# Cross-attention into a Winograd mixture layer on one core: a seventh product split once more, with placements, loads and transposes moved

## The chip, the cores and the metric

The kernel runs on one core of a Trainium2 chip. Its time is the device time of one execution in microseconds (us). The engines are TensorE (PE; PEld is its weight load), VectorE (DVE), ScalarE (ACT), GpSimd (POOL) and SyncE (SP), which here only issues DMAs. Each engine works through its own instructions in the order in which they were written; they meet only through semaphores. A DMA queue issues in order too.

## The reference

```python
x: (8, 8, 512, 64)   state: (8, 8, 32, 64)      # batch, head, tokens, features
scores = x @ state^T / 8;      a  = softmax(scores);   xread = a @ state
scores2 = state @ x^T / 8;     a2 = softmax(scores2);  sread = a2 @ x
t = concat([xread, sread], axis=tokens)                # (8, 8, 544, 64)
t = t.transpose(0, 2, 1, 3).reshape(4352, 512)
h = t @ w_in                                           # 512 x 2048
out = (h * sigmoid(h)) @ w_out                         # 2048 x 512
```

## The kernel before

The eight batches are worked through one after the other. For each batch b the 512 token rows of `xread` are never formed: W1[b] = state[b] @ w_in is made first (pieces of `ps_w`, line 479), and h = a @ W1[b] is sixteen tiles of 128 x 512 (`emit_G1`, line 546, two products of 512 columns each), put through SILU on ScalarE into `g` (line 574). The second matrix product, g @ w_out, is for batches 1 to 7 a Winograd form of Strassen's product: seven block products instead of eight, with p = 1 to 7 in `Unit.mm` (line 672), eight steps k of two 256-column products each. They need sums of halves of g on VectorE: `sums3` (in the code g's second half becomes a difference, in two instructions for k = 0 to 3 and 4 to 7), `sums2`, `sums1`, `sums4`; and differences of w_out, D1 to D4, made once (`t_weights`). Batch 0 uses plain products (`G2`, line 583). The last stage is the 256 rows of `sread`, at the end.

The seventh product (p = 7, the difference half of g with D3) is, for the batches named in INNER, split again by the same scheme (`inner_mm`, line 735): seven small products, each of four steps k of 128 columns. It needs four more sums of VectorE (`inner_sums`: t[2] from the first difference alone, t[0], t[1], t[3] from both), four weight differences made once in batch 1 (`inner_weights`, two on VectorE and two on GpSimd), and small copies and additions of VectorE that put the result together in `kept`. Inner product 1 reads only the first difference, 2 and 4 read the second.

The order within a batch is written out by hand. The loop over j (from 3 in batch 1 and 5 in the later ones, up to 15) emits h tile j, and `early(j)` puts behind it steps from the list `todo`, whose entries are (product, step, earliest j); products 1 and 7 are done there. At j = 5 and j = 9 the two differences of `sums3` are taken, and other VectorE work is put beside them. Then come products 2, 6, 4, 5 and 3, and between their steps the first five h tiles of the next batch (`units(3, {...})` says after which steps).

The attention of later batches is prepared ahead. With n = b + 1 and m = b + 2: x of batch m + 1 is loaded (`fetch_x`, on SP's queue), cast to bf16 by GpSimd (`cast_x`), transposed by a DMA (`transpose_x` into xT); scores of batch m are products (`scores_t`), exponentials on ScalarE (`exps_t`, into eT) are transposed by a DMA into e; `norm_t` sums them (reduction and reciprocal on VectorE), multiplies (half on GpSimd, half on VectorE), and `transpose_at` transposes the weights by a DMA into aT, which the h tiles of batch m read. Batch 2 is made in natural layout instead (`scores`, `exps`, `norm`, `transpose_a`). The states are loaded once, transposed by one DMA, and `evict_state` places them into stT, in four small copies for each half. State reads (`sread`) are done in groups, in batches 1, 4 and 6, normalised into xm, and transposed by DMAs (`transpose_xm`) for the last stage. `spread_x` copies x into the layout that the state reads take. ScalarE has to load a table whenever it changes between exponential and SILU.

Of the kernel before, what the change touches and what calls it, by code (L numbers as in the profile page):

```python
# [18 lines left out]
B = 8  # L19
# [23 lines left out]
def kernel(  # L43
# [8 lines left out]
    nc = tc.nc  # L52
# [58 lines left out]
    def load_x(b, h0=0, nh=H, eng=nc.gpsimd):  # L111
        eng.dma_start(
            x_f[b % 2][:, ds(h0, nh)],
            x[b, ds(h0, nh)].rearrange("h (p c) d -> p h c d", p=128, c=4)
        )
# [133 lines left out]
    def pe_transpose_x(b, hg, nb=2, new=bank, engs=(nc.vector, nc.scalar), only=None):  # L249
        if b not in xT:  # L250
            xT[b] = xtpool.tile([128, 4, 4, 128], BF16, tag="xT", name=f"xT{b}")
        m = 4 // nb
        for u in range(nb) if only is None else only:
            ps = new([128, m, 2, 128], BF16, "ps_xt")
            for i in range(m):
                for j in range(2):
                    nc.tensor.transpose(
                        ps[:, i, j, :],
                        x_nat[b][:, m * u + i, 2 * hg + j, :],
                        ident[:],  # L260
                    )
            copy(engs[u], xT[b][:, ds(m * u, m), ds(2 * hg, 2), :], ps[:])
# [23 lines left out]
    def evict_state(u, eng, b0, nb):  # L286
        to = stT.rearrange("p b k s (n m v) -> p b k s n m v", n=2, m=8)
        for g in range(2):
            for v in range(2):
                copy(  # L290
                    eng,
                    to[ds(64 * u, 64), ds(b0, nb), ds(2 * g, 2), u ^ g, :, :, v],
                    st_x[
                        ds(64 * v, 64), :, ds(b0, nb), ds(2 * g, 2), u, :
                    ].rearrange("p m b k n -> p b k n m"),
                )
# [62 lines left out]
    def norm_t(b):  # L359
        rs = att.tile([128, 2, 4, 4, 1], FP32, tag="rs2", name="rs2")  # L360
        rc = att.tile([128, 2, 4, 4, 1], FP32, tag="rcn", name="rcn")
        a = tpool.tile([128, 2, 4, 4, NS], BF16, tag="an2", name="an2")
        nc.vector.tensor_reduce(rs[:], e2[b][:], axis=AX, op=ADD)
        nc.vector.reciprocal(rc[:], rs[:])
        for hg, eng in enumerate((nc.gpsimd, nc.vector)):
            eng.tensor_tensor(
                a[:, hg], e2[b][:, hg], rc[:, hg].to_broadcast([128, 4, 4, NS]), op=MULT
            )
        return a

    def transpose_at(b, a):
        aT[b] = att.tile([128, 2, 4, 128], BF16, tag="aT", name="aT")
        nc.sync.dma_start_transpose(
            aT[b].rearrange("q g c p -> q (g c) p"), a.rearrange("p g c s n -> p (g c s n)")
        )
# [22 lines left out]
    def transpose_a(b, hg):  # L398
        nc.sync.dma_start_transpose(
            aT[b][:, hg, :, :], an[b, hg][:].rearrange("p c s n -> p (c s n)")  # L400
        )
# [174 lines left out]
    def G2(b, tt, ft):  # L576
        if ft == 0:
            if b == 0 and tt >= 2:
                outs[tt] = psA.tile([128, DM], FP32, tag=f"a{tt - 2}", name="o_a")
            else:  # L580
                i = 1 if b == B else tt % 2
                outs[tt] = psO.tile([128, DM], FP32, tag=f"o{i}", name="o")
        nc.tensor.matmul(  # L583
            outs[tt][:],
            gt[b * NFT + ft][:, ds(128 * tt, 128)],
            w_out_sb[:, ft, :],
            start=(ft == 0),
            stop=(ft == NFT - 1),
            skip_group_check=True,
        )  # L590
# [36 lines left out]
        }[which]  # L627
        sub(eng, d[which], a, c)

    INNER = (3, 4, 5, 6, 7)  # L630

    class Unit:
        def __init__(self, b):
# [262 lines left out]
    W0 = {2: (512, 512), 6: (1024, 512), 10: (1536, 512)}  # L896
    W1_AT = {2: 0, 6: 512}
    LEAD0 = [2, 3, 2, 2, 2, 3, 2, 1, 3, 3, 2, 3]
    T3 = {1: (0, 1), 2: (2,), 3: (3,), 4: (4,), 5: (5,), 6: (6,)}
    ready = 4  # L900
    for ft in range(12):
        upto(min(ft + LEAD0[ft], ready))
        if ft == 1:
            place_one_state(1, transpose_one_state(st1_n), nc.vector)
        if ft in W0:
            pss = w1_mms(0, [W0[ft]])
            if ft in W1_AT:
                pss1 = w1_mms(1, [(W1_AT[ft], 512)], new_h)
            w1_out(0, [W0[ft]], both, pss)
            if ft in W1_AT:  # L910
                w1_out(1, [(W1_AT[ft], 512)], both, pss1)
            ready = sum(W0[ft]) // 128
        if ft == 8:
            t_weights((1,), 0, 8)
        if ft == 9:
            t_weights((2, 3, 4), 0, 4)
        if ft == 11:
            for hg in range(2):
                cast_x(1, nc.gpsimd, 0, 2, 4 * hg, 4)
                cast_x(1, nc.vector, 2, 2, 4 * hg, 4)  # L920
            load_x(3)
            pe_transpose_x(1, 0, 1, engs=(nc.vector,))
            upto(16)
            nc.scalar.activation(warm[:], busy[:, 0:1], func=EXP, bias=0.0)
        for tt in range(3):
            G2(0, tt, ft)
            if ft == 7 and tt == 0:
                upto(9)
        for i in T3.get(ft, ()):
            G2(0, 3, i)  # L930
    pe_transpose_x(1, 1, 1, engs=(nc.vector,))
    G2(0, 3, 7)
    scores(1, 0, new=new_h)
    for ft in range(8, 12):
        G2(0, 3, ft)
    scores(1, 1, new=new_h)
    exps(1, 0)
# [48 lines left out]
    def fetch_x(i):  # L986
        n = 4 if i < 6 else H
        for h in range(0, H, n):
            load_x(i, h, n, nc.sync)

    for b in range(1, B):
        n = b + 1
        m = n + 1
        u = Unit(b)
        lead = 3 if b == 1 else LEADS
        inner = b in INNER
        if inner:
            todo = [(1, k - 8, k + 2) for k in range(6)] + [(7, 1, 9)]
            todo += [(7, 2, 10), (7, 4, 10), (7, 7, 11), (7, 6, 12), (7, 3, 13), (7, 5, 14)]
            todo += [(1, k - 8, 15) for k in (6, 7)]  # L1000
        else:
            last = 6
            todo = [(1, k - 8, k + 2) for k in range(last)]
            todo += [(7, k - 8, k + 4) for k in range(8)]
            todo += [(1, k - 8, k + 2) for k in range(last, 8)]
# [23 lines left out]
        for j in range(lead, NFT):  # L1029
            upto(NFT * b + j + 1)  # L1030
            if j == 8:
                u.hi = gh[b, 1]
            if j == max(lead, 5):
                u.sums3(0, 4)
                if b == 1:
                    t_weights((3,), 4, 4)
                    transpose_x(3)
                    for v in range(2):
                        evict_state(v, (nc.vector, nc.gpsimd)[v], 2, 2)
                if inner:  # L1040
                    u.inner_sums((3,))
                if 1 < b and m + 1 < B:
                    fetch_x(m + 1)
                if b == 2:
                    for v in range(2):
                        evict_state(v, (nc.vector, nc.gpsimd)[v], 4, 4)
            if j == 9:
                u.sums3(4, 4)
                if inner:
                    u.inner_sums((1, 2, 4))  # L1050
                if b == 1:
                    t_weights((2, 4), 4, 4)
                elif b == 2:
                    transpose_at(3, norm_t(3))
            early(j)
            if j == 13:
                u.sums2(0, 4)
        srs = SREAD_AT.get(b, ())

        def group_a():  # L1060
            pss = w1_next(PIECES_A[b])
            if m < B:
                scores_t(m)
            ps_sr = sread(srs, bank if m < B else new_h) if srs else None
            return pss, ps_sr
# [12 lines left out]
        if 2 < b < B - 1:  # L1078
            made = group_a()
# [3 lines left out]
        if 2 < b < B - 1:  # L1083
            xm = out_a()
# [23 lines left out]
            out_a()  # L1108
        if 1 < b and m < B:
            exps_t(m)  # L1110
        if b > 1 and srs:
            transpose_xm(srs, xm)
        step = 0

# [15 lines left out]
        if b == 1:  # L1130
            spread_x(2)
            for hg in range(2):
                norm(2, hg)
                transpose_a(2, hg)
            made = group_a()
            fetch_x(m + 1)
            exps_t(m)
            transpose_xm(srs, out_a())
        if m < B:
            nc.scalar.activation(warm[:], busy[:, 0:1], func=SILU, bias=0.0)  # L1140
        units(4)
# [20 lines left out]
        if b == 1:  # L1162
            group_b()
            for i in range(4):
                inner_weights(i, (nc.vector, nc.gpsimd)[i % 2])
        units(3, {2: 1, 3: 2, 5: 4, 7: 5} if b == 1 else {1: 2, 3: 3, 5: 4, 7: 5})
        if m + 1 < B:
            for c in range(4):
                cast_x(m + 1, nc.gpsimd, c, 1)
        if m == B:  # L1170
# [3 lines left out]
            normed = norm_t(m)  # L1174
        add(nc.vector, u.block(0, 1), u.block(0, 1), u.be[:])
        u.out_half(0)
        if m + 1 < B:
            transpose_x(m + 1)
        if 1 < b and m < B:
            transpose_at(m, normed)  # L1180
        for ft in range(NFT):
            gt.pop(NFT * b + ft)
    upto(NFT * B + NFT)
# [29 lines left out]
```

## Time and profile before

| | |
|---|---|
| median of 3 runs | 201.43 us (201.26 to 201.6) |
| profiled execution | 201.57 us, span 199.8 us |
| TensorE busy | 193.1 us, 97% of the span |
| VectorE busy | 157.1 us, 79% |
| ScalarE busy | 138.4 us, 69% |
| GpSimd busy | 72.7 us, 36% |
| mean granted TensorE clock | 0.998 of full speed |

Busy time is the sum of an engine's instructions. In the timelines, each line gives the start and the length in us from the start of the span, the engine, the line of the kernel, the operation, its output and inputs with their shapes, how many like it follow each other, and in square brackets how long the engine stood idle before it and what released it. Products overlap in TensorE's pipeline, so a line's length has some 0.16 us more than the distance to the next start; the distance between starts is what a product costs. VectorE's instructions overlap by about 0.08 us. In batch 2 product 2 begins near 69.7 us, in batch 3 at 91.59, in batch 4 at 113.14.

### The profile page before, as it was taken

The page shows a single profiled execution, that of the slowest core. Times are in us where ns is not written, and L with a number is a line of the kernel's source. Part 1 is how long each engine was busy: PE and PEld are TensorE (multiplying, and loading weights), DVE is VectorE, ACT ScalarE, POOL GpSimd, SP SyncE. Part 2 cuts the span into 40 slices and gives each one's busy share as a digit, 9 for nine tenths or more (in the row PEclk, how much of TensorE's full clock was granted, in tenths as well). Part 3 has the DMA queues.
Part 4 walks back from the last instruction along what each step waited for, and adds up shares of the span by engine and source line. Part 5 has one row for each costly group of instructions (what it writes and reads, how often), then busy time and mean ns, then how long its engine had stood idle before and what let it go on. Part 6 is the DMA issues. An engine that isn't in the chain of part 4 may idle for free.

```text
span 199.8 us, 4809 instructions
## 1 busy us (share of the span) xinstructions
PE 193.1 (97%) x1972; PEld 130.2 (65%) x1972; DVE 157.1 (79%) x289; ACT 138.4 (69%) x245; POOL 72.7 (36%) x93
## 2 busy tenths in 40 slices
PE   7799999999999999999999999999999999999992
PEld 2444445567766677667766777668666876788881
DVE  3852756997998999979998899989976997673072
ACT  3885657889777787889778957888588167825530
POOL 8664333750549803820273024602400226002200
PEclk9999999999999999999999999999999999999999
DMA  6999999993047998396229940842080005000042
GB/s 195 190 206 206 247 262 347 246 256 81 5 131 204 239 229 168 149 233 198 53 105 193 260 93 10 282 90 53 12 252 3 3 13 210 3 0 0 39 176 105
DMA packets 40822, 28.72 MB, mean 144 GB/s; under 512 B 27360, under 2 KB 37472, under 8 KB 40800
## 3 DMA queue, kind: packets, MB, share of 16 engines
q1 hardware_dynamic: 34592, 20.52, 39.2%
q0 software_dynamic: 5920, 7.64, 18.4%
q8 instruction: 15, 0.25, 0.5%
q10 hardware_dynamic: 288, 0.26, 0.4%
q14 instruction: 7, 0.06, 0.1%
HBM read 17.43 MB, written 8.91 MB: 132 GB/s over the span
## 4 chain that ended last, share of the span: by engine, by line
PE 85%; DMA 7%; DVE 5%; POOL 0%; issue 0%; POOLq 0%; DVEq 0%
PE o L672 34%; PE h L546 25%; PE ps_w L479 4%; DMA w_in_sb<-in_moe_w_in_dram 4%; PE h L564 3%; PE o L583 3%; PE o_a L583 3%; DMA xT<-x_nat 3%; PE o L735 2%; DVE g L597 2%; PE o_s L793 2%; PE o_ch L735 2%; PE o L793 1%; PE ps_sr L423 1%; DVE stT L162 1%; PE ps_scT L336 1%
## 5 line engine op out<-in xcount | busy, mean ns | idle before, releaser
L574 ACT ACTIVATE g<-h 128x512 bf16<-128x512 f32 (+1 forms) x142 | 79.9, 573 | 32.4 <-PE h L546 20.9
L546 PE MATMUL h<-aT,W 128*128 128x512 bf16 x252 | 72.9, 379 | 0.1
L672 PEld LDWEIGHTS <-g 128*128 128x128 bf16 x480 | 46.3, 98 | 22.4 <-DVE kept L600 0.7
L672 PE MATMUL o<-w_out_sb,g 128*128 128x256 bf16 x336 | 48.7, 273 | 0.1
L600 POOL TENSOR_TENSOR o_sb<-o_sb,kept 128x512 f32<-128x512 f32 x7 | 9.7, 1392 | 70.6 <-ACT o_sb L160 61.4
L546 PEld LDWEIGHTS <-W 128*128 128x128 bf16 x252 | 23.2, 98 | 7.9 <-issue 0.9
L672 PE MATMUL o<-wt,s 128*128 128x256 bf16 x224 | 27.3, 273 | 0.0
L162 DVE CAST W<-ps_w 128x512 bf16<-128x512 f32 (+1 forms) x35 | 21.7, 666 | 6.2 <-PE ps_w L479 6.2
L672 PEld LDWEIGHTS <-s 128*128 128x128 bf16 x224 | 21.5, 98 | 4.3 <-issue 1.9
L160 ACT ACTIVATE W<-ps_w 128x512 bf16<-128x512 f32 (+1 forms) x31 | 16.4, 583 | 6.5 <-PE ps_w L479 6.5
L672 PE MATMUL o<-wt,g 128*128 128x256 bf16 x144 | 19.4, 273 | 0.0
L600 POOL TENSOR_TENSOR o_sb<-kept,o_sb 128x512 f32<-128x512 f32 x7 | 9.0, 1284 | 24.8 <-ACT o_sb L160 24.8
L162 POOL CAST x_nat<-x_f 128x512 bf16<-128x512 f32 x24 | 17.5, 768 | 1.5 <-DMA x_f<-in_x_dram 1.5
L597 DVE TENSOR_TENSOR g<-g 128x1024 bf16<-128x1024 bf16 x15 | 14.6, 970 | 2.8 <-ACT g L574 2.6
L600 DVE TENSOR_TENSOR o_sb<-o_sb,o 128x512 f32<-128x512 f32 x14 | 9.5, 680 | 9.1 <-PE o L672 6.9
L160 ACT ACTIVATE o_sb<-o 128x512 f32<-128x512 f32 x15 | 8.9, 595 | 9.7 <-PE o L672 5.4
L597 DVE TENSOR_TENSOR g<-g,s 128x1024 bf16<-128x1024 bf16 x14 | 13.8, 1027 | 0.0
L597 DVE TENSOR_TENSOR s<-g 128x512 bf16<-128x512 bf16 (+3 forms) x23 | 11.0, 508 | 0.0
L479 PE MATMUL ps_w<-w_in_sb,stT 64*32 64x512 bf16 (+1 forms) x264 | 10.2, 375 | 0.4 <-DMA w_in_sb<-in_moe_w_in_dram 0.4
L583 PEld LDWEIGHTS <-g 128*128 128x128 bf16 x64 | 5.8, 98 | 7.0 <-issue 0.8
L583 PE MATMUL o_a<-w_out_sb,g 128*128 128x512 bf16 x32 | 10.0, 379 | 0.0
L600 DVE TENSOR_TENSOR s<-s,g 128x1024 bf16<-128x1024 bf16 x15 | 9.7, 684 | 0.0
(122 smaller groups left out, 251.8 us busy)
## 6 DMA issues: line engine op xcount, KB each, us to landing
out_dram<-o_sb SPq DMA_DIRECT2D x14, 512.0 KB, 2.7
x_f<-in_x_dram SPq DMA_DIRECT2D x6, 512.0 KB, 4.9
x_f<-in_x_dram POOLq DMA_DIRECT2D x2, 1024.0 KB, 11.4
x_f<-in_x_dram SPq DMA_DIRECT2D x2, 1024.0 KB, 6.7
w_out_sb<-in_moe_w_out_dram POOLq DMA_DIRECT2D x6, 256.0 KB, 11.2
w_in_sb<-in_moe_w_in_dram POOLq DMA_DIRECT2D x3, 512.0 KB, 10.8
x_f<-in_x_dram POOLq DMA_DIRECT2D x2, 512.0 KB, 14.5
out_dram<-o_sb SPq DMA_DIRECT2D x4, 256.0 KB, 5.4
```

The source lines that it names most:

```text
L160: nc.scalar.activation(dst, src, func=COPY, bias=0.0)
L162: eng.tensor_copy(dst, src)
L479: nc.tensor.matmul(pss[f, hg][ds(32 * s, 32), 0:n], stT[ds(r, 64), b, h // 2, s % 2, :], w_in_sb[ds(r, 64), h // 2, ds(f, n)], start=True, ...
L546: nc.tensor.matmul(h_ps[k][:], W1[b][:, hg, ds(128 * ft, 128)], aT[b][:, hg, :, :], start=(hg == 0), stop=(hg == 1), skip_group_check=True,)
L564: nc.tensor.matmul(ps[:, 0:256], w_in_sb[:, kt, ds(128 * ft, 128)], xmT[:, :, kt].rearrange("p t n b -> p t (n b)"), start=(kt == 0), stop ...
L574: nc.scalar.activation(gt[k], ps[:, 0:n], func=SILU, bias=0.0)
L583: nc.tensor.matmul(outs[tt][:], gt[b * NFT + ft][:, ds(128 * tt, 128)], w_out_sb[:, ft, :], start=(ft == 0), stop=(ft == NFT - 1), skip_gr ...
L597: eng.tensor_tensor(dst, a, c, op=SUB)
L600: eng.tensor_tensor(dst, a, c, op=ADD)
L672: nc.tensor.matmul(to[:, t, :], left[:, ds(128 * t, 128)], right[:, k, :], start=first and t == 0, stop=(k == 7), skip_group_check=True,)
L735: nc.tensor.matmul(to, left[:, k], right[:, k], start=where not in self.begun, stop=(k == 3), skip_group_check=True,)
L793: nc.tensor.matmul(to[:, 0:n], left[:, k], right[:, k, ds(c, n)], start=(first and k == 0), stop=(k == 7), skip_group_check=True,)
```

## The change

- INNER gets batch 2, so its seventh product is split as well. Batch 2 has a `todo` of its own: four steps of product 1, the seven inner products, then the other four steps of product 1.
- The states of batches 4 to 7 are placed in batch 1 at j = 9, all eight copies by GpSimd, instead of in batch 2 at j = 5, four by VectorE and four by GpSimd.
- `norm_t(3)` and its transposes move in batch 2 from j = 9 (behind the second difference) to j = 5 (ahead of it). On VectorE the order becomes: first difference, t[2], reduction, reciprocal, multiplication, second difference, the three other inner sums.
- x of batch 4 is fetched at j = 13 of batch 1, cast behind batch 2's normalisation, and transposed there, instead of at the end of batch 1. In that place the scores' transposes of batch 3 (in `exps_t`) now stand ahead of those of batch 2's weights.
- The transposes of the state reads of batches 1 and 4 are issued at the end of their batch, behind its stores.
- In batch 0 the product (token block 3, step 7) moves up to step 10 of the loop, and the product (block 0, step 11) ahead of the transposes of x of batch 1.
- In batch 1 the first two h tiles of batch 2 come after steps 3 and 4 of product 3, instead of after steps 2 and 3.

```diff
-    INNER = (3, 4, 5, 6, 7)
+    INNER = (2, 3, 4, 5, 6, 7)
...
-    T3 = {1: (0, 1), 2: (2,), 3: (3,), 4: (4,), 5: (5,), 6: (6,)}
+    T3 = {1: (0, 1), 2: (2,), 3: (3,), 4: (4,), 5: (5,), 6: (6,), 10: (7,)}
...
             load_x(3)
+            G2(0, 0, 11)
             pe_transpose_x(1, 0, 1, engs=(nc.vector,))
...
-        for tt in range(3):
+        for tt in range(ft == 11, 3):
...
-        if inner:
+        if b == 2:
+            todo = [(1, k - 8, k + 2) for k in range(4)] + [(7, 1, 9)]
+            todo += [(7, 2, 10), (7, 4, 10), (7, 7, 11), (7, 6, 12), (7, 3, 12), (7, 5, 13)]
+            todo += [(1, k - 8, (k + 24) // 2) for k in range(4, 8)]
+        elif inner:
...
                 if b == 2:
-                    for v in range(2):
-                        evict_state(v, (nc.vector, nc.gpsimd)[v], 4, 4)
+                    transpose_at(3, norm_t(3))
             if j == 9:
                 u.sums3(4, 4)
                 if inner:
                     u.inner_sums((1, 2, 4))
                 if b == 1:
                     t_weights((2, 4), 4, 4)
-                elif b == 2:
-                    transpose_at(3, norm_t(3))
+                    for v in range(2):
+                        evict_state(v, nc.gpsimd, 4, 4)
             early(j)
             if j == 13:
                 u.sums2(0, 4)
+                if b == 1:
+                    fetch_x(4)
...
-        if b > 1 and srs:
+        if m == B:
             transpose_xm(srs, xm)
...
             for hg in range(2):
                 norm(2, hg)
+            for c in range(4):
+                cast_x(4, nc.gpsimd, c, 1)
+            made = group_a()
+            exps_t(m)
+            for hg in range(2):
                 transpose_a(2, hg)
-            made = group_a()
-            fetch_x(m + 1)
-            exps_t(m)
-            transpose_xm(srs, out_a())
+            transpose_x(4)
+            xm = out_a()
...
-        units(3, {2: 1, 3: 2, 5: 4, 7: 5} if b == 1 else {1: 2, 3: 3, 5: 4, 7: 5})
-        if m + 1 < B:
+        units(3, {3: 1, 4: 2, 5: 4, 7: 5} if b == 1 else {1: 2, 3: 3, 5: 4, 7: 5})
+        if 1 < b and m + 1 < B:
             for c in range(4):
                 cast_x(m + 1, nc.gpsimd, c, 1)
...
-        if m + 1 < B:
+        if 1 < b and m + 1 < B:
             transpose_x(m + 1)
         if 1 < b and m < B:
             transpose_at(m, normed)
+        if srs and m < B:
+            transpose_xm(srs, xm)
```

More of the change, by code (lines that the diff above doesn't have):

```diff
@@ L931 @@
     pe_transpose_x(1, 1, 1, engs=(nc.vector,))
-    G2(0, 3, 7)
+    G2(0, 3, 8)
     scores(1, 0, new=new_h)
-    for ft in range(8, 12):
+    for ft in range(9, 12):
         G2(0, 3, ft)
```

## The prediction

> **What bounds the kernel now.** I read the page first (engine shares, clock, chain), then the timelines of TensorE, VectorE and GpSimd, batch by batch.
>
> ```profile
> PE 193.1 (97%) x1972; PEld 130.2 (65%) x1972; DVE 157.1 (79%) x289; ACT 138.4 (69%) x245; POOL 72.7 (36%) x93
> PE 85%; DMA 7%; DVE 5%; POOL 0%; issue 0%; POOLq 0%; DVEq 0%
> ```
>
> TensorE is full, and the chain of waits runs mostly through it; the granted clock is 1.00 in every batch. So I compare each start on TensorE's timeline with the start before it plus the work between (four 256-column products 0.44 us, two of 512 columns 0.43, eight of 128 columns 0.45). What is left over between 16 us and the end of batch 2, apart from some 0.09 wherever the kind of product changes, is mainly: 0.22 before 27.33 and 0.14 before 28.34 (batch 0); 0.15 and 0.11 around 57.99 (the first h of batch 2 waits for aT); 0.36 between 71.49 and 72.29 (xT of batch 4). TensorE lines of batches 2 and 3:
>
> ```profile
> 64.42 0.59 PE L546 MATMUL h<-aT,W 128*128 128x512 bf16 x2
> 64.85 0.60 PE L672 MATMUL o<-wt,g 128*128 128x256 bf16 x4
> 65.28 0.59 PE L546 MATMUL h<-aT,W 128*128 128x512 bf16 x2
> ...
> 72.29 0.41 PE L336 MATMUL ps_scT<-xT,stT 64*32 64x512 bf16 x8 [0.17 <-DMA xT<-x_nat]
> 72.63 1.92 PE L672 MATMUL o<-wt,s 128*128 128x256 bf16 x16
> ...
> 86.36 0.59 PE L546 MATMUL h<-aT,W 128*128 128x512 bf16 x2
> 86.79 0.61 PE L735 MATMUL o<-wt,g 128*128 128x128 bf16 x8
> ```
>
> VectorE in the same stretch:
>
> ```profile
> 61.18 0.69 DVE L600 TENSOR_TENSOR o_sb<-o_sb,o 128x512 f32<-128x512 f32 x1 [0.72 <-PE o L672]
> 61.79 1.46 DVE L597 TENSOR_TENSOR g<-g 128x1024 bf16<-128x1024 bf16 x1
> 63.17 2.49 DVE L162 COPY stT<-st_x 64x128 bf16<-64x128 bf16 x4
> 65.70 0.85 DVE L597 TENSOR_TENSOR g<-g 128x1024 bf16<-128x1024 bf16 x1
> 66.47 1.21 DVE L363 TENSOR_REDUCE rs<-e 128x32 f32<-128x1024 bf16 x1
> 67.71 0.35 DVE L364 RECIPROCAL rcn<-rs 128x32 f32<-128x32 f32 x1
> 68.10 0.69 DVE L366 TENSOR_TENSOR an<-e,rcn 128x512 bf16<-128x512 bf16 x1
> ...
> 85.45 1.25 DVE L597 TENSOR_TENSOR g<-g 128x1024 bf16<-128x1024 bf16 x1 [0.21 <-ACT g L574]
> 86.73 0.43 DVE L600 TENSOR_TENSOR inner<-g 128x512 bf16<-128x512 bf16 x1
> ```
>
> From 61.18 VectorE has no idle time until 85.24. It is not the engine of the chain, but in batch 2 it has no room. The lines at 85.45 and 86.79 show what the split product needs: the second difference (upper half of g, call its end S) ends at 86.70, and the second inner product starts at 86.79. The unsplit product of batch 2 needs it only at its fifth step, after 66.36.
>
> GpSimd:
>
> ```profile
> 57.18 1.27 POOL L600 TENSOR_TENSOR o_sb<-kept,o_sb 128x512 f32<-128x512 f32 x1 [1.26 <-ACT o_sb L160]
> 60.20 2.50 POOL L597 TENSOR_TENSOR wt<-wt,wt 128x512 bf16<-128x512 bf16 x2 [1.75 <-DVE wt L597]
> 62.70 2.84 POOL L162 CAST x_nat<-x_f 128x512 bf16<-128x512 f32 x4
> 65.60 2.09 POOL L162 COPY stT<-st_x 64x128 bf16<-64x128 bf16 x4
> ```
>
> **The change part by part.** The profiled execution took 201.57 us (span 199.8 and 1.77 around it); the median is 201.43, 0.14 less. I sum on the profiled one.
>
> *Batch 0.* Two 0.22 us products move into the gaps of 0.22 and 0.14, so TensorE is 0.36 ahead from 28.9. But two h tiles behind them start 0.07 later (0.22 into a gap of 0.14), and the next hard step is not TensorE's: ScalarE loads the exponential table at 30.53, straight after the SILU of these tiles, exponentials run 31.94 to 33.10, normalised weights are ready at 34.71 (GpSimd) and 35.26 (VectorE), and TensorE takes them at 34.89 and 35.33, the second at once. So the lead is waited away: +0.07 us. Ends -0.36 (all kept) and +0.1.
>
> *Placing states 4 to 7 on GpSimd.* VectorE loses four copies (63.17 to 65.66, 2.5 us). GpSimd does eight from 42.98 instead, by its rows 0.49 us each, to 47, in idle time that lasts to 52.20. Beside GpSimd a 128x1024 subtraction takes 1.09 us (39.68), alone 0.69 (43.09). Three lie there: +1.2 us of VectorE, of which its idle 1.09 before 46.20 takes most; the first would end near 44.2, and TensorE wants it at 44.27. I take 0; ends 0 and +0.3.
>
> *x of batch 4 sooner.* Two loads go to SP near 45 instead of 57.2, where SP is idle; the buffer was freed by 37.7. The four casts (2.84 us) now follow the two normalisations (end 55.9), so the GpSimd sum of 57.18 starts near 58.8 and ends near 60.1; VectorE's sum at 61.18 reads what it wrote, still in time, and the two weight differences on GpSimd keep 60.2. xT leaves at 59 instead of 65.57, lands (6.7 us then) by 66, and the 0.36 wait goes; no wait takes its place, as its reader comes after 71. It can now stand before both stores, the three state-read transposes (4.2 us of SP), x of batch 5 and aT of batch 3 on SP; the last is then issued near 70 and, at 6.3 us, lands by 76.3, needed near 80. If SP were 4 us later still, batch 3 would wait.
>
> *e before aT on SP.* eT is complete at 53.1, so its transpose (1.24 us of SP) is through before the first aT can go (GpSimd ends it at 54.67). As the first h now comes one step later (0.22), the 0.26 of waiting is about gone: h of step 5 ends near 61.63 instead of 61.78, VectorE's sum starts at 61.05 (with batch 0's +0.07). Ends: 0.26 gained; 0.5 lost, if aT lands behind e, which took 5.3 us.
>
> *State reads' transposes last* (batches 1 and 4): 4.2 to 4.6 us of SP moved behind the stores; they feed only the last batch. 0.
>
> *Split seventh product of batch 2.* 16 products of 256 columns (1.75 us) become 28 of 128 (1.57): -0.18 on TensorE. The Trainium skill (TensorE: The Clock Gate, Back-to-back issue gap) gives about 81 ns per 128-column product with its weight load in a stream; by that, 28 cost 2.27 us, and this term is an estimated +0.52. Rows here say 56 ns (0.45 for eight, at 86.79), so the trace disagrees with it.
>
> What it costs is order on VectorE: batch 3's normalisation now stands *between* the two differences, and the second inner product waits for the second. From 61.05, with starts counted to the next start:
> - sum 0.61; first difference 1.25 (0.61 alone, 1.38 here beside GpSimd); one inner difference 0.5 (0.45 to 0.71);
> - reduction 1.24, reciprocal 0.39, multiplication 0.8 (0.61 to 1.0; GpSimd does the other half beside it);
> - second difference 1.0 (0.77 to 1.25).
>
> S = 66.85; all short 65.7, all long 67.6 (rounded up). I take middles because GpSimd is busy to 62.7 and from 65, but not between.
>
> TensorE gets there earlier: only four steps of product 1 now precede, so ScalarE sets the pace (0.6 us per tile), and the h pair of step 10 ends near 65.0. It then stands for 1.9 us, with nothing behind it allowed to pass. After S: 0.09, two inner products 0.45, five h pairs 2.17, four inner products 0.90, four steps of product 1 0.87: product 2 starts at S + 4.48. (Batch 3: 86.70 to 90.73 with two such steps, 4.03; two more, 0.44.) Product 2 with 0.09 takes 1.84, pieces and scores 0.77: product 6 starts at S + 7.1 = 73.95, against 72.63. So +1.3. VectorE's inner work (1.4 of sums, some 2.5 of copies and additions with its waits) replaces 2.5 of placements and a 0.6 copy, so VectorE too enters batch 3 late: adding its rows from S, at 85.05 against 83.44, and there it costs another 0.05 to 0.1. From batch 3 on nothing is idle to give it back.
>
> Sum: 201.57 + 1.27 + 0.08 = 202.9 on the profiled execution (batch 0 and aT are in 61.05); less 0.14, **202.8** against the median of 201.43.
>
> **Rivals.**
> - *R1, faster: the wait is covered.* If the second difference ended before 65.0, TensorE would not stand: -0.18, -0.36, -0.26, +0.07, i.e. 200.7. For it: 2.5 us of copies really leave this place. Against: 3.0 us come in (0.5 + 2.4), and even all short ends give 65.7. S must be 0.7 below every row. Chance 0.11.
> - *R2, no change:* short ends, S near 65.9, and part of batch 0's lead kept: 201.5. Chance 0.09.
> - *R3, more:* differences held at their long ends beside GpSimd, S 67.5, placements stalling batch 1 by 0.2, or aT behind e: 203.7. For it: 1.46 at 61.79. Against: GpSimd idles from 62.7. Chance 0.17.
> - *R4: 128-column products at the slower pace.* Taking 0.08 us for each, 0.7 more than the term above, largely behind the wait: 203.2. Against: 0.45 for eight in five batches. Chance 0.03. The page named above is the rule for it.
> - *The forecast:* 202.8, own range 202.2 to 203.4. Chance 0.60.
>
> **How the numbers follow.** A difference under 0.2% (0.4 us) can't be told from none. Slower: 0.60 + 0.17 + 0.03 = 0.80; same 0.09; faster 0.11. The range leaves out most of R1 and the far end of R3: 201.4 to 203.9.
>
> **What would show it.** In batch 2, TensorE's second inner product waits 1 to 2.4 us for VectorE, behind the reduction and the multiplication; it starts within 0.1 us of the end of the second difference. No wait at the scores of batch 4; 28 inner products at 56 ns; the products moved in batch 0 fill both gaps, but the wait returns near 34.8. Wrong if the reduction stands elsewhere on VectorE in effect, if the differences run near 0.6, or if later batches have idle time to absorb a late start.

## The result, and the profile after

The changed kernel takes 203.69 us (median of 6 runs, 203.62 to 204.44) against 201.51 us for the kernel before (6 runs on the same chip). The ratio is 1.0113, with a 95% interval of 1.0093 to 1.0133: it is slower by 1.1%, some 2.2 us. The forecast was 202.8, with a range of 201.4 to 203.9 and 0.80 for slower. The direction and the place were right; the size was short. The time lies within the whole range, near its upper end, but outside the forecast's own 202.2 to 203.4: it is the time of the rival R3.

The page of the changed kernel, engine shares and chain of waits:

```profile
PE 193.9 (96%) x1984; PEld 130.2 (65%) x1984; DVE 157.8 (78%) x294; ACT 138.3 (69%) x245; POOL 74.8 (37%) x97
PE 82%; DVE 9%; ACT 2%; POOL 2%; DMA 1%; issue 1%; SPq 0%; POOLq 0%; DVEq 0%
```

VectorE is hardly busier than before (157.8 us for 157.1), but its share of the chain went from 5 to 9%. TensorE's timeline says where (first two lines of the kernel before, then the changed kernel):

```profile
57.99 0.70 PE L546 MATMUL h<-aT,W 128*128 128x512 bf16 x2
58.53 0.38 PE L672 MATMUL o<-w_out_sb,g 128*128 128x256 bf16 x2
```

```profile
58.12 0.38 PE L546 MATMUL h<-aT,W 128*128 128x512 bf16 x1
58.93 0.38 PE L546 MATMUL h<-aT,W 128*128 128x512 bf16 x1 [0.44 <-DMA aT<-an]
...
65.44 0.59 PE L546 MATMUL h<-aT,W 128*128 128x512 bf16 x2
67.52 0.62 PE L735 MATMUL o<-wt,g 128*128 128x128 bf16 x8 [1.49 <-DVE g L597]
67.97 0.59 PE L546 MATMUL h<-aT,W 128*128 128x512 bf16 x2
...
74.21 0.40 PE L336 MATMUL ps_scT<-xT,stT 64*32 64x512 bf16 x8
74.54 1.92 PE L672 MATMUL o<-wt,s 128*128 128x256 bf16 x16
```

The second inner product (67.52) stands 1.65 us behind the end of the h pair before it. The scores of batch 4 (74.21) no longer wait for xT. Product 6 starts at 74.54, 1.91 us later than before (72.63). VectorE in the same stretch:

```profile
61.78 0.69 DVE L600 TENSOR_TENSOR o_sb<-o_sb,o 128x512 f32<-128x512 f32 x1 [1.26 <-PE o L672]
62.38 0.92 DVE L597 TENSOR_TENSOR g<-g 128x1024 bf16<-128x1024 bf16 x1
63.34 0.42 DVE L597 TENSOR_TENSOR inner<-g 128x512 bf16<-128x512 bf16 x1
63.68 1.21 DVE L363 TENSOR_REDUCE rs<-e 128x32 f32<-128x1024 bf16 x1
64.93 0.35 DVE L364 RECIPROCAL rcn<-rs 128x32 f32<-128x32 f32 x1
65.32 0.69 DVE L366 TENSOR_TENSOR an<-e,rcn 128x512 bf16<-128x512 bf16 x1
65.93 1.53 DVE L597 TENSOR_TENSOR g<-g 128x1024 bf16<-128x1024 bf16 x1
67.50 0.42 DVE L600 TENSOR_TENSOR inner<-g 128x512 bf16<-128x512 bf16 x1
```

The reduction, the reciprocal and the multiplication stand between the two differences, and the second difference takes 1.53 us. For its first 0.98 us it lies beside GpSimd's half of the multiplication:

```profile
65.36 1.55 POOL L366 TENSOR_TENSOR an<-e,rcn 128x512 bf16<-128x512 bf16 x1 [2.60 <-DVE rcn L364]
```

That half ends at 66.91, and the second difference 0.55 us later. Alone such a difference takes 0.69, so it would have ended near 66.6 (an estimate); some 0.8 of TensorE's 1.65 us is then GpSimd's half, and the rest the order on VectorE. No run kept the order and took GpSimd's half away.

What TensorE gained and lost up to product 6, read from starts as in the prediction:

| | us |
|---|---|
| batch 0: first h of batch 1 at 36.48, before at 36.42 | +0.06 |
| wait for aT 0.59, before 0.26 | +0.33 |
| ScalarE's pace (the profile names no releaser; ScalarE is busy without a gap beside them): 0.19 before 61.07, 0.19 before 65.17, 0.05 before 65.44 | +0.43 |
| wait for the second difference | +1.65 |
| split product, 28 of 128 columns at 56 ns | -0.18 |
| wait for xT gone | -0.36 |
| sum (measured +1.91) | +1.93 |

From product 6 to product 2 of batch 3 another 0.15 us comes to it (an h tile waits until 81.69); product 2 of batch 3 is 2.06 late (93.65 for 91.59), and the span ends 2.0 late (201.8 for 199.8).

### The profile page after: what moved, and what is told of

It is laid out like the page before. It is cut to its first block, busy times and chain, and to the rows that moved or that the text cites. A ratio compares the mean times of both kernels' runs of the same rounds, so it can differ in the third digit from the quotient of the medians.

```text
span 201.8 us, 4841 instructions
## 1 busy us (share of the span) xinstructions
PE 193.9 (96%) x1984; PEld 130.2 (65%) x1984; DVE 157.8 (78%) x294; ACT 138.3 (69%) x245; POOL 74.8 (37%) x97
## 4 chain that ended last, share of the span: by engine, by line
PE 82%; DVE 9%; ACT 2%; POOL 2%; DMA 1%; issue 1%; SPq 0%; POOLq 0%; DVEq 0%
PE o L672 31%; PE h L546 25%; PE ps_w L479 4%; PE h L564 3%; PE o L735 3%; PE ps_busy L168 3%; PE o L583 3%; PE o_a L583 2%; DVE g L597 2%; PE o_ch L735 2%; POOL an L389 2%; PE o_s L793 2%; PE o L793 1%; DMA aT<-an 1%; DVE s L600 1%; DVE o_sb L600 1%
## 5 line engine op out<-in xcount | busy, mean ns | idle before, releaser
L672 PEld LDWEIGHTS <-g 128*128 128x128 bf16 x464 | 44.8, 98 | 21.3 <-issue 1.1
L672 PE MATMUL o<-wt,g 128*128 128x256 bf16 x128 | 16.8, 273 | 0.0
L597 DVE TENSOR_TENSOR g<-g 128x1024 bf16<-128x1024 bf16 x15 | 14.0, 935 | 2.5 <-ACT g L574 2.4
L597 DVE TENSOR_TENSOR g<-g,s 128x1024 bf16<-128x1024 bf16 x14 | 14.9, 1102 | 0.0
L735 PEld LDWEIGHTS <-inner 128*128 128x128 bf16 x96 | 7.3, 98 | 5.5
L583 PEld LDWEIGHTS <-g 128*128 128x128 bf16 x64 | 5.8, 98 | 7.0 <-issue 0.8
```

Source lines behind the costliest of these rows:

```text
L583: nc.tensor.matmul(outs[tt][:], gt[b * NFT + ft][:, ds(128 * tt, 128)], w_out_sb[:, ft, :], start=(ft == 0), stop=(ft == NFT - 1), skip_gr ...
L597: eng.tensor_tensor(dst, a, c, op=SUB)
L672: nc.tensor.matmul(to[:, t, :], left[:, ds(128 * t, 128)], right[:, k, :], start=first and t == 0, stop=(k == 7), skip_group_check=True,)
L735: nc.tensor.matmul(to, left[:, k], right[:, k], start=where not in self.begun, stop=(k == 3), skip_group_check=True,)
```

## The experiments

Three theories were set against each other: **A**, the order on VectorE is the cost; **B**, the amount of VectorE's work is, and the order only chooses where TensorE stands; **C**, the order of DMAs on SP is the cost. In the runs below, "the mark" is TensorE's first transpose of batch 1's weights (34.89 us before, 34.83 after). Traces differ in what lies ahead of it (the mark lies between 34.54 in e10 and 35.12 in e7), so product 6 is counted from there: 37.74 us before, 39.71 after.

**e1: the normalisation behind the inner products**

```diff
-                if b == 2:
-                    transpose_at(3, norm_t(3))
...
             early(j)
+            if j == 13 and b == 2:
+                transpose_at(3, norm_t(3))
```

> The changed kernel, with batch 3's normalisation behind the seven inner products (step 13 of batch 2) instead of between the two differences. Theory A (the order on VectorE is what costs): the second difference ends near 65.5, the 1.65 us wait of TensorE at the second inner product is gone, nothing else waits, 202.0 us. Theory B (the amount of VectorE work is what costs, the order only chooses where TensorE waits): the wait in batch 2 goes as well, but VectorE leaves batch 2 no earlier than some 0.6 to 1 us before the changed kernel does, and TensorE waits for its differences in batch 3: 202.7 to 203.1 us. Theory C (the DMA order alone costs): no change, 203.7.

Measured: 204.01 us, ratio 1.0133 (1.0106 to 1.0160). The wait at the second inner product is gone, as A and B had it, and yet nothing is gained. TensorE's line and two of VectorE's:

```profile
74.23 1.91 PE L672 MATMUL o<-wt,s 128*128 128x256 bf16 x16 [1.54 <-DVE kept L162]
```

```profile
69.79 1.21 DVE L363 TENSOR_REDUCE rs<-e 128x32 f32<-128x1024 bf16 x1
72.03 1.54 DVE L597 TENSOR_TENSOR s<-g 128x1024 bf16<-128x1024 bf16 x1
```

The same wait now stands ahead of product 6: it is released by a copy of VectorE (73.50), which stands behind the three instructions and behind a sum that takes 1.54 beside GpSimd. Product 6 still starts a little earlier than in the changed kernel, 39.46 from the mark; that is lost again in batch 3, where TensorE waits for an addition of VectorE:

```profile
81.17 0.60 PE L672 MATMUL o<-w_out_sb,g 128*128 128x256 bf16 x4 [0.44 <-DVE o_sb L600]
```

A falls. B was right that the wait moves and that some of it shows in batch 3, but wrong that most of it would be there and that 0.6 to 1 us would come back.

**e2: the normalisation in batch 1, while VectorE waits**

```diff
-        if 1 < b and m < B:
+        if m < B:
             normed = norm_t(m)
...
                 if b == 2:
-                    transpose_at(3, norm_t(3))
+                    transpose_at(3, normed)
```

> The changed kernel, with batch 3's normalisation at the end of batch 1, ahead of the last sum there, in the 1.26 us in which VectorE waits for TensorE; its transpose stays where it was. Theory A: the second difference ends near 65.9, just when TensorE asks, 202.1 us. Theory B: the same time, because 1.26 us of idle time of VectorE are filled, so that batch 3 starts in time too; if the run e1_norm_late is clearly slower than this one, B holds and A doesn't. Theory C: 203.7.

Measured: 202.07 us, ratio 1.0020 (0.9983 to 1.0057). VectorE:

```profile
60.51 1.22 DVE L363 TENSOR_REDUCE rs<-e 128x32 f32<-128x1024 bf16 x1
62.15 1.24 DVE L366 TENSOR_TENSOR an<-e,rcn 128x512 bf16<-128x512 bf16 x1
...
65.22 0.68 DVE L597 TENSOR_TENSOR g<-g 128x1024 bf16<-128x1024 bf16 x1
```

The reduction runs in what was idle time, the second difference ends at 65.90 (65.9 was expected) and takes 0.68. Product 6 is 38.20 from the mark. Since e1 is clearly slower than this run, moving the work into idle time helps and merely moving it does not. C falls as the main cause: e still stands ahead of aT here, and most of the loss is gone.

**e3: aT ahead of e on SP**

```diff
-            exps_t(m)
+            turn_e = exps_t(m, True)
             for hg in range(2):
                 transpose_a(2, hg)
+            turn_e()
...
```

Here `exps_t(m, True)` leaves the transpose out, and `turn_e` issues it.

> The changed kernel, with the transposes of batch 2's weights (aT) ahead of the one of batch 3's exponentials (e) on SP, as before the change. If e ahead of them is what made aT late: the second product of batch 2's first h tile waits for 0.0 to 0.15 us instead of 0.44, VectorE's sum starts near 61.1 instead of 61.78 and everything behind follows: 203.0 us. If the one step later, the earlier casts on GpSimd or the other traffic did it: aT still lands near 58.9, and 203.6 us. e may then be late itself: it lands near 60 or 61 and is needed at 63.

Measured: 204.68 us (203.37 to 205.59), ratio 1.0165 (1.0107 to 1.0224): a miss. The wait for aT is gone, but another came ahead of it. TensorE:

```profile
57.87 1.03 PE L676 MATMUL o<-w_out_sb,g 128*128 128x256 bf16 x8 [0.45 <-DVE o_sb L604]
58.74 0.59 PE L550 MATMUL h<-aT,W 128*128 128x512 bf16 x2
```

The sum that it waits for ran at 57.14, in the changed kernel at 56.45. In this run x of batch 2 landed late (GpSimd's casts start at 36.60, in the changed kernel at 35.03), GpSimd's placements lasted until 49.5 instead of 47.8, and VectorE's half sums beside them took longer:

```profile
48.29 0.96 DVE L601 TENSOR_TENSOR s<-g 128x512 bf16<-128x512 bf16 x2
49.17 1.49 DVE L604 TENSOR_TENSOR s<-s,g 128x1024 bf16<-128x1024 bf16 x2
```

(0.75 and 1.28 in the changed kernel.) Of the 0.69 us by which the sum is late, 0.43 arise in these two lines. So the wait goes with e's place, but the run says nothing on the price; e7 and e10 take that up. Its four executions spread from 203.37 to 205.59 us, and only the one of 204.01 was profiled. The two longest have a mean granted clock of 0.988 and 0.992, near the 0.989 to 0.991 of e5's three longest (see the last section); what happened in them is not shown.

**e4: the product unsplit, all moves kept**

```diff
-    INNER = (2, 3, 4, 5, 6, 7)
+    INNER = (3, 4, 5, 6, 7)
...
-        if b == 2:
-            todo = [(1, k - 8, k + 2) for k in range(4)] + [(7, 1, 9)]
...
-        elif inner:
+        if inner:
```

> The changed kernel with batch 2 out of INNER and its list of steps as before; placements, loads, transposes and the normalisation stay moved. Theory A and B: the unsplit product asks for the second difference only at its fifth step, near 67.0, about when it is there; VectorE has 3.3 us less to do, and the wait shrinks to 0.2 us or less; what stays is aT (0.6) less the xT wait that is gone (0.36): 201.7 us. Theory C, or if the moves themselves cost: above 202.5.

Measured: 202.18 us, ratio 1.0040 (1.0019 to 1.0061). TensorE and VectorE:

```profile
59.21 0.38 PE L546 MATMUL h<-aT,W 128*128 128x512 bf16 x1 [0.68 <-DMA aT<-an]
```

```profile
69.36 0.69 DVE L162 COPY kept<-o 128x512 f32<-128x512 f32 x1 [2.31 <-PE o L672]
```

Here VectorE waits for TensorE, for 2.31 us, and in batch 2 TensorE no longer for VectorE: without the split there is room. Some 1.5 us of the loss belong to the split in this order. The moves that stay are still 0.4% slower than the kernel before; the waits that show are that for aT, 0.83 us in this trace, and 0.19 of ScalarE's pace.

**e5: only the split**

```diff
-    INNER = (3, 4, 5, 6, 7)
+    INNER = (2, 3, 4, 5, 6, 7)
...
-        if inner:
+        if b == 2:
+            todo = [(1, k - 8, k + 2) for k in range(4)] + [(7, 1, 9)]
...
+        elif inner:
```

> The kernel before, with only batch 2's seventh product split (with the changed kernel's list of steps); states 4 to 7 are still placed in batch 2 at step 5, the normalisation still stands at step 9, behind the inner sums. Theory B (amount of VectorE work in batch 2): 2.7 us more than before, and in none of its idle time, so TensorE is late by 2.7 us and up to 1 us more of VectorE's own waits: 204.2 to 205.2 us, more than the changed kernel, whose moved placements took 2.5 us away. Theory A (only what stands between the two differences counts): the placements stand there as the normalisation did, 2.5 against 2.3 us: 203.5 to 203.9.

Measured: 207.32 us (205.8 to 207.34), ratio 1.0272 (1.0233 to 1.0311), above both. TensorE stands twice, at the second inner product (behind the placements) and at the fifth in order, which needs the first one's result copied out (the copy stands behind the normalisation):

```profile
67.14 0.62 PE L735 MATMUL o<-wt,g 128*128 128x128 bf16 x8 [1.71 <-DVE g L597]
...
71.13 0.38 PE L735 MATMUL o_ch<-wt,inner 128*128 128x128 bf16 x4 [2.28 <-DVE kept L162]
...
71.72 1.06 PE L546 MATMUL h<-aT,W 128*128 128x512 bf16 x2
```

Then its clock drops, which no theory had: see the last section. Product 6 is 43.39 from the mark, 5.65 later than before, 1.7 of it by the clock; the changed kernel is 1.97 late. So the moves of the change take half of this price away even without the clock.

**e6: only x of batch 4 sooner** (aT stays ahead of e)

```diff
             if j == 13:
                 u.sums2(0, 4)
+                if b == 1:
+                    fetch_x(4)
...
+            for c in range(4):
+                cast_x(4, nc.gpsimd, c, 1)
             made = group_a()
-            fetch_x(m + 1)
             exps_t(m)
+            transpose_x(4)
...
```

> The kernel before, with only x of batch 4 fetched, cast and transposed in batch 1; aT stays ahead of e on SP, the placements and all else stay. If the 0.36 us wait for xT was worth its length: no wait at the scores of batch 4, 201.1 us. If VectorE, which is busy without a gap there, takes its place: 201.4 us.

Measured: 201.26 us (12 runs), before 201.39; ratio 0.9996 (0.9977 to 1.0015). The wait for xT is gone and product 6 is 37.35 from the mark, 0.39 earlier than before. Of this 0.24 is left at product 2 of batch 3. The time doesn't tell the two apart.

**e7: only e ahead of aT**

```diff
             for hg in range(2):
                 norm(2, hg)
-                transpose_a(2, hg)
             made = group_a()
-            fetch_x(m + 1)
             exps_t(m)
+            for hg in range(2):
+                transpose_a(2, hg)
+            fetch_x(m + 1)
```

> The kernel before, with only the order on SP turned: e of batch 3 ahead of aT of batch 2. If e ahead of aT makes aT land later: TensorE's wait at the first h tile of batch 2 grows from 0.26 us to some 0.8; VectorE's sum starts that much later, but the 0.36 us wait for xT swallows a part: 201.7 us, at most 202.1. If it does nothing: 201.4, and the wait of 0.59 us in the changed kernel has another cause.

Measured: 201.74 us, before 201.39; ratio 1.0003 (0.9983 to 1.0023). TensorE, then SP in this run, in the changed kernel and in the kernel before:

```profile
59.26 0.38 PE L546 MATMUL h<-aT,W 128*128 128x512 bf16 x1 [0.67 <-DMA aT<-an]
```

```profile
53.38 2.08 SPq L352 DMA_TRANSPOSE e<-eT  x1
55.56 2.53 SPq L399 DMA_TRANSPOSE aT<-an  x2
```

```profile
53.21 1.96 SPq L352 DMA_TRANSPOSE e<-eT  x1
55.26 2.53 SPq L399 DMA_TRANSPOSE aT<-an  x2
```

```profile
54.49 2.64 SPq L399 DMA_TRANSPOSE aT<-an  x2
```

The wait is 0.98 us, 0.15 before the tile and 0.83 in it (0.26 in all before; 0.8 was expected). SP takes 2 us to issue e's transpose here, not 1.24, and the first aT starts 0.8 to 1.1 later. By product 6 (38.06 from the mark) 0.32 of it is left, because the xT wait is gone; the times do not tell the two apart.

**e8: only batch 0's two products**

```diff
-    T3 = {1: (0, 1), 2: (2,), 3: (3,), 4: (4,), 5: (5,), 6: (6,)}
+    T3 = {1: (0, 1), 2: (2,), 3: (3,), 4: (4,), 5: (5,), 6: (6,), 10: (7,)}
...
+            G2(0, 0, 11)
             pe_transpose_x(1, 0, 1, engs=(nc.vector,))
...
-        for tt in range(3):
+        for tt in range(ft == 11, 3):
...
-    G2(0, 3, 7)
+    G2(0, 3, 8)
...
-    for ft in range(8, 12):
+    for ft in range(9, 12):
```

> The kernel before, with only the two products of batch 0 moved. As in the prediction: TensorE is 0.36 us ahead from 29 us, waits for the normalised weights near 34.8, and the first products of batch 1 start within 0.1 us of the kernel before: 201.4 us. If the lead were kept: 201.05.

Measured: 201.45 us, before 201.39; ratio 0.9998 (0.9979 to 1.0016). From the h tiles that stand between the two moved products to the first h of batch 1 it is 9.16 us (27.04 to 36.20), in the kernel before 9.09 (27.33 to 36.42): the lead is waited away.

**e9: both halves of the multiplication on GpSimd**

```diff
-        for hg, eng in enumerate((nc.gpsimd, nc.vector)):
+        for hg, eng in enumerate((nc.gpsimd, nc.gpsimd if b == 3 else nc.vector)):
```

> The changed kernel, with both halves of batch 3's multiplication on GpSimd, which idles there: VectorE does one instruction less between the two differences (0.69, start to next start 0.61), the order is else unchanged. Theory B (VectorE's work from 61.8 us on sets TensorE's time, microsecond by microsecond): the second difference ends 0.6 us earlier, near 66.9, unless GpSimd, now busy beside it for its whole length, makes the difference itself longer (1.53 in the changed kernel, 0.69 alone); 203.1 us, or 203.7 if it does. If the amount isn't what counts: 203.7 with the second difference earlier.

Measured: 203.56 us, ratio 1.0112 (1.0078 to 1.0147): no gain. TensorE, VectorE and GpSimd:

```profile
66.19 0.61 PE L735 MATMUL o<-wt,g 128*128 128x128 bf16 x8
...
69.00 0.38 PE L735 MATMUL o_ch<-wt,inner 128*128 128x128 bf16 x4 [1.33 <-DVE kept L162]
```

```profile
65.29 0.63 DVE L597 TENSOR_TENSOR g<-g 128x1024 bf16<-128x1024 bf16 x1
65.95 1.15 DVE L600 TENSOR_TENSOR inner<-g 128x512 bf16<-128x512 bf16 x1
67.13 1.15 DVE L597 TENSOR_TENSOR inner<-inner,g 128x512 bf16<-128x512 bf16 x1
```

```profile
65.45 2.56 POOL L366 TENSOR_TENSOR an<-e,rcn 128x512 bf16<-128x512 bf16 x2 [2.63 <-DVE rcn L364]
```

The difference starts ahead of GpSimd's multiplications, keeps its length and ends at 65.92, a microsecond ahead of the 66.9 that was expected. But the two inner sums take 1.15 us each beside GpSimd (0.42 in the changed kernel), and TensorE stands 1.33 later on, at the fifth inner product in order. So GpSimd does lengthen VectorE's path, only at other instructions than the text had expected.

**e10: e2 with aT ahead of e**, the edits of e2 and e3 together

> Run e2_norm_early with aT ahead of e on SP. TensorE no longer waits for aT at 58 us (0.59 in the changed kernel). Theory B: VectorE works from 57.4 without a gap that TensorE could shorten, the second difference still ends near 65.9, and the time is that of e2, 202.1 us. If TensorE's own lateness were still part of the loss: 201.6.

Measured: 202.06 us (12 runs), before 201.53; ratio 1.0029 (1.0012 to 1.0045). TensorE:

```profile
57.94 0.59 PE L550 MATMUL h<-aT,W 128*128 128x512 bf16 x2
...
65.70 0.62 PE L739 MATMUL o<-wt,g 128*128 128x128 bf16 x8 [0.23 <-DVE g L601]
```

No wait for aT any more, and no gain: product 6 is 38.19 from the mark, 38.20 in e2, and the ratios (1.0029 and 1.0020) can't be told apart. The 0.43 us that TensorE gains at 58 us it waits for VectorE again, about half at the first inner product (64.64; the first difference ends at 64.58) and half at the second.

**e11: e6 with the placements on GpSimd**

```diff
-                if b == 2:
-                    for v in range(2):
-                        evict_state(v, (nc.vector, nc.gpsimd)[v], 4, 4)
...
                     t_weights((2, 4), 4, 4)
+                    for v in range(2):
+                        evict_state(v, nc.gpsimd, 4, 4)
```

> Run e6_x4_sooner with states 4 to 7 placed by GpSimd in batch 1, batch 2's product unsplit: the two moves of the change that take waits and VectorE work away, without the split and without e ahead of aT. Placements alone: VectorE gets 2.4 us of idle time in batch 2 that nothing asks for, so the time is that of e6, 201.2 us, at best 201.0; if GpSimd's eight copies in batch 1 hold up VectorE's sums there, 201.5 to 202.

Measured: 201.39 us (12 runs), before 201.53; ratio 0.9993 (0.9980 to 1.0006). VectorE now has time to spare in batch 2:

```profile
64.17 0.69 DVE L597 TENSOR_TENSOR g<-g 128x1024 bf16<-128x1024 bf16 x1 [0.91 <-ACT g L574]
...
68.53 0.69 DVE L162 COPY kept<-o 128x512 f32<-128x512 f32 x1 [1.43 <-PE o L672]
```

Product 6 is 37.35 from the mark, as in e6. No version was found that beats the kernel before by more than can be measured.

## Why the prediction was right, and where it was off

*The mechanism* held: TensorE waits at the second inner product for the second difference, which stands behind the reduction and the multiplication. From the start of VectorE's sum to the end of the second difference the prediction counted 5.80 us; it took 5.68 (61.78 to 67.46). From there to product 6 it counted 7.1; it took 7.08. The first of these agreements is partly luck. The second difference took 1.53 for 1.0, more than the 1.25 that the sum had as its longest, because GpSimd's half of the multiplication still ran when it started. The first difference took 0.96 for 1.25, since GpSimd was about done when it came, and the first inner sum and the multiplication together 0.35 less than counted. TensorE's wait was 1.65 for 1.9.

*The term that was off* is "e before aT on SP", where the text has e's transpose through SP in 1.24 us before the first aT can go, and the waiting about gone. SP took 1.96, the first aT left at 55.26 (54.67 counted) and the second at 56.6 (55.9 before), and the wait grew from 0.26 to 0.59. The issue time of e is not all of it, as SP's lines of e2 show:

```profile
53.17 1.23 SPq L352 DMA_TRANSPOSE e<-eT  x1
54.52 3.19 SPq L399 DMA_TRANSPOSE aT<-an  x2
```

There e took 1.23 and the first aT left at 54.52, as before the change, but the second only at 56.5, and TensorE still waited 0.43. With e ahead the wait within that tile was 0.43 to 0.87 (e1, e2, e4, e7, e9), with aT ahead none (e10). Why the second aT leaves late stays open.

So VectorE's sum started at 61.78 and not at 61.05, and everything that hangs on it came 0.73 later; of that, the aT wait makes about 0.59, and 0.19 is ScalarE's pace at 61.07, which the sum had only for the later steps. The end that was kept for it, 0.5 lost, held. Of the 0.9 us between 202.8 and 203.7 it accounts for some 0.6 (product 6 at 74.54 for 73.95); this is worked out from the trace, since e3, which was to show it, ran into another wait. Alone (e7) its price can't be measured, and with the normalisation moved (e10) taking the wait away gains nothing. The sum also has 1.27 where its own rows give 1.32 (73.95 less 72.63), too little to matter.

*Smaller terms.* Batch 0: +0.06 for +0.07, and e8 shows why. The 128-column products: eight in 0.45 us, 56 ns each. The Trainium skill's figure that was weighed, 81 ns (TensorE: Matmul & The Clock Gate, Back-to-back issue gap), does not hold for this stream. The wait for xT: gone, as counted, in the changed kernel and in e6. Placements on GpSimd: 0 in the changed kernel, but in e3 they ended 1.7 us later, and TensorE waited 0.45 for a sum that had become late, mostly beside them; R3 had 0.2 for that. Batch 3: 0.15 for 0.05 to 0.1, but the same 0.15 stands in e6 and e11, where batch 2 is shorter than before, so the reason that the prediction gave for it is not shown.

*The rivals.* R1 needed the second difference before 65.0; even with the normalisation out of the way (e2) it ended at 65.9. R3, with a chance of 0.17, gave 203.7, and that is the time. Of its three causes aT behind e occurred. The second difference's end at 67.5 occurred too (67.46), but by the late start: the two differences together took 2.49 for 2.25. The placements cost nothing. R4 did not occur.

*What decides, then.* The table counts VectorE from its last instructions of batch 1 (59.6 to 59.9 us, the weight differences) to the end of the sums that product 6 reads, idle time taken out by the brackets of the timeline. Work includes the time that an instruction is drawn out by GpSimd:

| | work, us | idle in it, us | product 6 from the mark | time, us |
|---|---|---|---|---|
| before | 11.1 | 0.7 | 37.74 | 201.51 |
| after | 11.6 | 2.3 | 39.71 | 203.69 |
| e1 | 11.9 | 3.3 | 39.46 | 204.01 |
| e9 | 11.2 | 2.6 | 39.57 | 203.56 |
| e2 | 11.2 | 1.1 | 38.20 | 202.07 |
| e10 | 11.2 | 1.1 | 38.19 | 202.06 |
| e4 (unsplit) | 8.4 | 3.8 | 38.21 | 202.18 |

VectorE's work in the changed kernel is only 0.5 us more than before: the 2.5 us that left made room for what came. So B, the amount, falls too in its plain form; A fell with e1, and C with e2. With the split, what counts is the path through VectorE: its work and the idle time that the order forces on it, 1.26 us behind TensorE at 61.78 and 1.06 inside the inner products. Of the runs with the split only e2 and e10, which put work into the first of these, are faster. This account was made after the runs, and e2 against e1 is what supports it. The changed kernel, e2, e9 and e10 fit it (product 6 starts 0.88 us behind the sums' end in each), while in e1 product 6 starts 0.61 before that end, so its row does not add up in the same way. In e4, where VectorE waits for TensorE, its idle time costs nothing. Not settled is the last 0.5 us by which e10 stays behind the kernel before: its trace still has TensorE waiting for VectorE at the first two inner products (0.25 and 0.39 by starts), and ScalarE's pace before that, but no run took these away alone.

## What to carry to other kernels

When work on an in-order engine is moved, follow the engine from the last point where something holds it to the next value that the full engine asks for, and count the idle time on that path as well as the work: the same three instructions cost 1.65 us in one place, about as much in a second, and almost nothing in a third, where the engine was waiting anyway. The transpose of e that was put ahead of aT on the DMA queue made aT late in every trace that had it so. Its issue took 1.24 to 2.70 us in the kernel before; take the longest row for the bad end of a range, not the shortest alone. And handing the other half of the multiplication to GpSimd gained nothing (e9), because GpSimd then ran beside other instructions on VectorE's path. An addition or difference of VectorE that comes while GpSimd works is better counted from GpSimd's end (0.54 to 0.55 us behind it for 128x1024 here) than by its own length.

## What the runs showed of the hardware

*TensorE's clock fell to a half after two waits.* In e5 TensorE stood 1.71 and then 2.28 us within 6 us. Each line has a stretch of the span and its length, then the busy time and the instructions of TensorE, its weight loads, VectorE, ScalarE and GpSimd, then the granted clock and two columns on DMA:

```profile
71.00:72.00 1.00, 0.87 (x9) 0.74 (x9) 0.36 (x2) 0.00 (x0) 0.78 (x1) 0.70 1.07 231
72.00:73.00 1.00, 1.00 (x7) 0.57 (x5) 0.00 (x0) 0.19 (x1) 0.00 (x0) 0.50 0.86 269
73.00:74.00 1.00, 1.00 (x5) 0.44 (x4) 0.73 (x3) 0.41 (x1) 0.00 (x0) 0.50 0.86 247
74.00:75.00 1.00, 1.00 (x7) 0.61 (x5) 0.96 (x3) 0.60 (x1) 0.00 (x0) 0.60 1.09 343
75.00:76.00 1.00, 1.00 (x10) 0.80 (x9) 0.41 (x2) 0.60 (x1) 0.00 (x0) 1.00 1.32 192
```

The clock is 0.50 from about 71.4 to 74.8, and an h pair took 0.85 us instead of 0.43 (71.72 to 72.57). That is some 1.7 us lost on top of the waits, an estimate, as half of 3.4. In the changed kernel, with one wait of 1.65 us, the clock stayed at 1.00 in every stretch from 58 to 80 us. The Trainium skill (TensorE: Matmul & The Clock Gate, Part 1: The HAM clock gate) has half rate after an idle window of about 3.4 us and full rate after as long a busy one; the second agrees with this trace, while here the clock fell with no idle stretch longer than 2.28 us; whether that wait alone or both together did it was not tried.

*VectorE beside GpSimd.* A subtraction of 128x1024 took 0.69 us alone and 1.53 when GpSimd's multiplication was running at its start; a 128x512 one 0.42 and 1.15 (e9). How long it takes follows from when GpSimd ends: in the changed kernel the first difference ended 0.54 us behind GpSimd's instruction (63.30 and 62.76) and the second 0.55 (67.46 and 66.91), in e1 the sum at 72.03 0.54 (73.57 and 73.03), in e4 the second difference 0.55 (67.05 and 66.50), whatever the overlap was. So in these rows VectorE's instruction got little done until GpSimd's had ended. A difference that started first, in e9 at 65.29, kept its length (0.63). The reduction took 1.20 to 1.22 in every run, with GpSimd busy beside it (e2, at 60.51) or idle (e1, at 69.79).
